# Ranks of the polynomial exponential steps, the load limit at the layer boundary and the end stop in a planned attention kernel

## Chip, cores, metric

One core of a Trainium2 chip. The metric is the device time of one execution in microseconds (us). All executions quoted are fast; a change counts as faster or slower from 2% on, and the text gives each ratio with its 95% interval. Ratios are the mean time of one kernel's fast runs over that of the kernel before in the same rounds, so not quite the ratio of the medians that are quoted.

## The reference

Two layers, each an attention block and a squared-ReLU MLP, with the same weights in both layers.

```python
B, S, D, F, H = 1, 2048, 448, 1792, 16          # Dh = 28, bf16 inputs
def attn(x):   # qkv = x @ wqkv, per head softmax(q k^T / sqrt(28)) v, then @ wo
def mlp(x):    # relu(x @ w1 + b1)**2 @ w2 + b2
x = x + attn(layernorm(x));  x = x + mlp(layernorm(x))     # layer 0
x = x + attn(layernorm(x));  x = x + mlp(layernorm(x))     # layer 1
```

## The kernel before

The kernel is written by a planner that runs at build time. Every piece of work (`Op`) has an engine, an assumed duration, dependencies and buffers; streams of such pieces have a rank. The planner takes the piece that can start first, and at equal starts the one with the smaller rank (a further rule, left out here, keeps TensorE free for scores that are due). The chip then runs each engine's pieces in that order.

```python
class Planner:
    def run(self):
        while self.streams:
            ...   # cands: (start, rank, engine, stream) of each stream's next piece
            s, _, e, st = min(cands, key=lambda c: (max(c[3][2].ready, self.clock[c[2]])
                     if c[2] == "PE" and self.turns() else c[0], c[1]))
            ...
```

Scores are cut into units of 128 keys x 512 columns: 2048 units in two layers. A group of three units goes to ScalarE's exponential. A fourth unit may be taken by VectorE, which computes the exponential by a polynomial in six steps.

```python
    def apart(i, now, us):            # may a unit go to VectorE here?
        if len(units) - i < STOP or not LEAD <= len(gbuf) <= LAST:
            return None
        ...                           # a scratch set free? a result buffer? keys ready?
        if pl.load(SPAN, "DVE") > (BB if l == 0 and qb == len(blocks[0]) - 1
                                   or l == 1 and units[i][0] < bridged else BUSY):
            return None               # BB = 0.5, BUSY = 0.95, SPAN = 12 us
        ...
    def a_unit(gi, x, src, unit, l):
        ...
        # the first step; its stream has a rank of its own, 1.5, which the change leaves
        c = Op("DVE", 0.69, take, deps=[("s", gi)], acq=sets_of(unit), rel=x)
        yield c
        pl.spawn(V_PRIO, a_rest(gi, c, box, unit, (b0, b1, b2, b3)))   # V_PRIO = 3.8
    def a_rest(gi, c, box, unit, bs):  # four polynomial steps and the power of two
        ...
```

The "row blocks" are the work on 256 rows once their attention is done: output projection, layernorm, MLP, and, in layer 0, a second layernorm and layer 1's queries, keys and values. Their stream has the rank 4 + 0.1 x block; its evictions (copies of matmul results), statistics and squares have rank 3.5.

```python
            pl.spawn(... else 4 + 0.1 * qb, chain(l, qb))
    def layernorm(...):
        ...                            # rstd on GpSimd
        nm = Op("DVE", 0.42, norm, deps=[rss[j]], ...)   # has the row block's rank
        ...                            # transposes on TensorE, then copies of xnT on VectorE
```

At the layer boundary ("the bridge") layer 1's attention starts on row blocks 0 to 2 with the keys that exist, before layer 0's last row blocks are finished; its last passes need the keys of row blocks 6 and 7.

The softmax here doesn't subtract the row's maximum and nothing guards it: scores larger than these inputs give would overflow.

## Time and profile before

| | before |
|---|---|
| median | 919.29 us when the change was predicted, 918.57 us over four runs |
| exponentials on ScalarE, units on VectorE | 652, 93 |
| start of the first and last exponential | 11.3 and 896.8 us of a span of 918.8 us |
| from the last exponential's start to the end ("tail") | 22.0 us |
| ScalarE idle in front of exponentials ("gaps") | 5.5 us |
| VectorE busy, 390 to 575 us | 120.5 us, 65% |

In a group line the columns are line, engine, operation, output and inputs, count, then busy time and mean duration in ns, then the idle time in front and who ended it. In a table by stretches each row gives the stretch, its length, and busy time and count of the engines named in the text. In a line of waits they are the piece that waited, what it waited for, the sum in us, the number of times and the longest. In a list in order of time they are start and duration in us, engine, line, operation, shapes and count; in brackets stands the idle time before.

### The profile page before, as it was taken

The page shows a single profiled execution, that of the slowest core. Times are in us where ns is not written, and L with a number is a line of the kernel's source. Part 1 is how long each engine was busy: PE and PEld are TensorE (multiplying, and loading weights), DVE is VectorE, ACT ScalarE, POOL GpSimd, SP SyncE. Part 2 cuts the span into 40 slices and gives each one's busy share as a digit, 9 for nine tenths or more (in the row PEclk, how much of TensorE's full clock was granted, in tenths as well). Part 3 has the DMA queues.
Part 4 walks back from the last instruction along what each step waited for, and adds up shares of the span by engine and source line. Part 5 has one row for each costly group of instructions (what it writes and reads, how often), then busy time and mean ns, then how long its engine had stood idle before and what let it go on. Part 6 is the DMA issues. An engine that isn't in the chain of part 4 may idle for free.

```text
span 918.8 us, 30455 instructions
## 1 busy us (share of the span) xinstructions
PE 842.7 (92%) x13606; PEld 483.0 (53%) x13606; DVE 698.9 (76%) x1433; ACT 887.3 (97%) x672; POOL 42.6 (5%) x89
## 2 busy tenths in 40 slices
PE   8999988999989999899999999888989999899998
PEld 4555545455455455455555455545445545555565
DVE  7755589799799788986667556788898978998454
ACT  5999999999999999999999999999999999999992
POOL 5100000000000000000000100000000000000000
PEclk9999999999999999999999999999999999999999
DMA  7200010000000000000000000011000000000100
GB/s 219 73 2 2 2 35 24 14 9 14 15 13 9 14 14 8 14 14 2 1 2 2 2 1 2 3 39 38 20 13 14 24 20 15 22 14 19 28 6 22
DMA packets 32992, 18.53 MB, mean 20 GB/s; under 512 B 17498, under 2 KB 32411, under 8 KB 32860
## 3 DMA queue, kind: packets, MB, share of 16 engines
q1 hardware_dynamic: 32860, 16.58, 6.3%
q8 instruction: 106, 1.74, 0.8%
q14 instruction: 26, 0.21, 0.1%
HBM read 14.26 MB, written 2.07 MB: 18 GB/s over the span
## 4 chain that ended last, share of the span: by engine, by line
ACT 66%; issue 13%; PE 11%; DVE 6%; DMA 3%; SPq 0%; POOL 0%; POOLq 0%; ACTq 0%
ACT pt L769 66%; PE mt L523 4%; PE sc L751 3%; DMA dn<-oT_sb 3%; PE oT L909 2%; PE sc L523 1%; DVE v_h L837 1%; DVE st L416 1%; DMA V_sb<-in_A_wqkv_dram 1%; DVE K_sb L837 1%; PE tp L462 0%; DVE xn L489 0%; DVE oT_sb L933 0%; DVE v_e L832 0%; DVE v_i L822 0%
## 5 line engine op out<-in xcount | busy, mean ns | idle before, releaser
L769 ACT ACTIVATE pt<-sc 128x1536 bf16<-128x1536 f32 x652 | 876.7, 1616 | 5.5 <-PE sc L751 4.0
L751 PE MATMUL sc<-Q_sb,K_sb 32*128 32x256 bf16 (+1 forms) x6288 | 334.5, 266 | 57.9 <-ACT pt L769 54.1
L751 PEld LDWEIGHTS <-K_sb 32*128 32x128 bf16 x6598 | 172.8, 92 | 228.8 <-issue 221.9
L909 PE MATMUL oT<-pt,V_sb 128*32 128x256 bf16 (+1 forms) x4164 | 150.3, 269 | 1.1 <-ACT pt L769 0.5
L909 PEld LDWEIGHTS <-V_sb 128*32 128x32 bf16 x4352 | 93.2, 96 | 47.2 <-issue 41.3
L523 PE MATMUL mt<-xnT,w 128*128 128x256 bf16 (+1 forms) x888 | 114.9, 271 | 1.1 <-DVE rec L960 0.3
L523 PEld LDWEIGHTS <-w 128*128 128x128 bf16 x952 | 79.8, 98 | 31.4 <-issue 22.3
L1041 DVE TENSOR_SCALAR r<-mt 128x512 bf16<-128x512 f32 x105 | 72.0, 686 | 24.4 <-PE mt L523 23.8
L837 DVE SCALAR_TENSOR_TENSOR K_sb<-K_sb 128x512 f32<-128x512 uint16 x132 | 90.1, 683 | 0.4
L837 DVE SCALAR_TENSOR_TENSOR v_h<-v_h,v_i 128x512 f32<-128x512 f32 x98 | 66.7, 681 | 0.3
L1003 DVE TENSOR_TENSOR x_sb<-x_sb,mt 128x448 bf16<-128x448 bf16 (+2 forms) x63 | 38.1, 605 | 27.1 <-PE mt L523 26.6
L1092 PE MATMUL mt<-xn,ident 128*128 128x448 bf16 x154 | 51.8, 356 | 3.4 <-DVE v_i L822 1.1
L523 PE MATMUL mt<-w,h 128*128 128x448 bf16 x224 | 51.9, 354 | 0.0
L751 PE MATMUL mt<-Q_sb,K_sb 32*128 32x256 bf16 x310 | 49.3, 270 | 0.8 <-DVE x_sb L1003 0.8
L438 POOL TENSOR_TENSOR ve<-mv,eps_t 128x2 f32<-128x2 f32 (+1 forms) x34 | 9.2, 272 | 858.9 <-DVE mv L417 858.9
L822 DVE TENSOR_SCALAR v_i<-mt 128x512 int32<-128x512 f32 x49 | 33.7, 687 | 16.4 <-PE mt L751 16.1
L523 PE MATMUL mt<-w,V_sb 128*128 128x448 bf16 (+2 forms) x210 | 45.0, 342 | 0.0
L416 DVE BATCH_NORM_STATS2 st<-x_sb 128x6 f32<-128x448 bf16 x64 | 39.6, 619 | 1.3 <-DMA x_sb<-in_A_x_dram 0.7
L931 DVE COPY oT_sb<-oT 128x256 f32<-128x256 f32 (+1 forms) x48 | 19.1, 397 | 27.7 <-PE oT L909 27.6
L822 DVE TENSOR_SCALAR K_sb<-mt 128x512 int32<-128x512 f32 x44 | 30.1, 685 | 10.7 <-PE mt L751 10.6
L837 DVE SCALAR_TENSOR_TENSOR v_h<-v_i 128x512 f32<-128x512 uint16 x49 | 33.5, 685 | 0.5
L541 DVE TENSOR_SCALAR Q_sb<-mt 128x512 bf16<-128x512 f32 (+1 forms) x31 | 21.0, 678 | 16.4 <-PE mt L523 16.4
(97 smaller groups left out, 736.4 us busy)
## 6 DMA issues: line engine op xcount, KB each, us to landing
rec<-scr SPq DMA_DIRECT2D x56, 128.0 KB
x_sb<-in_A_x_dram SPq DMA_DIRECT2D x8, 224.0 KB
out_dram<-x_sb SPq DMA_DIRECT2D x15, 112.0 KB
w<-in_B_w_dram SPq DMA_DIRECT2D x1, 1568.0 KB
w<-in_B_w_dram SPq DMA_DIRECT2D x1, 1344.0 KB
dn<-oT_sb SPq DMA_DIRECT2D x56, 4.0 KB
scr<-dn SPq DMA_DIRECT2D x56, 4.0 KB
V_sb<-in_A_wqkv_dram SPq DMA_DIRECT2D x1, 672.0 KB
```

What stands on the lines that cost most here:

```text
L416: nc.vector.bn_stats(out=st[:, :], in_=x_sb[:, t0 + j, :])
L523: nc.tensor.matmul(box["t"][:, c0:c0 + n], lhsT=lhsT() if callable(lhsT) else lhsT, rhs=rhs, start=a, stop=b)
L541: nc.vector.tensor_scalar(out=dst, in0=src, scalar1=by, scalar2=None, op0=ALU.mult)
L751: nc.tensor.matmul(dst[k][:, i * nt * P:(i + 1) * nt * P], lhsT=K_sb[l][rows, g, (kb + i) * P:(kb + i + 1) * P], rhs=Q_sb[rows, g, t0 * P: ...
L769: nc.scalar.activation(out=pt[:, 0:n], in_=gbuf[gi]["sc"][:, 0:n], func=AF.Exp, scale=float(np.log(2.0)) * 2.0 ** -FRAC)
L822: nc.vector.tensor_scalar(out=box["i"], in0=two(src), scalar1=EXP_BIAS, scalar2=EXP_LOW, op0=ALU.add, op1=ALU.max)
L837: nc.vector.scalar_tensor_tensor(out=box["h"], in0=box["f"] if begin else box["h"], scalar=b, in1=box["f"], op0=ALU.add, op1=ALU.mult)
L909: nc.tensor.matmul(box["t"][DHP * hh:DHP * hh + DHP, 0:n], lhsT=V_sb[l][:, kb + i, 4 * g + hh, :], rhs=p[:, c0:c0 + n], start=begin and kb ...
L931: nc.vector.tensor_copy(out=dst, in_=src)
L1003: nc.vector.tensor_tensor(out=x_sb[:, tb, lo:hi], in0=x_sb[:, tb, lo:hi], in1=t[:, 0:hi - lo], op=ALU.add)
L1041: nc.vector.tensor_scalar(out=r[:, 0:w], in0=t[:, 0:w], scalar1=0.0, scalar2=None, op0=ALU.max)
L1092: nc.tensor.matmul(t[:, 0:D], lhsT=ident[:, :], rhs=xns[0][:, 0:D], start=True, stop=True)
```

## The change

Its intent: let VectorE take more units where it is half idle, at the layer boundary (BB, the limit on VectorE's planned load over the last 12 us) and near the end (STOP, the number of units before the end from which on VectorE takes none), and keep their polynomial steps from delaying the row blocks: rank 6 instead of 3.8, and 3.0 once a unit is 5 us old.

```diff
-BB = 0.5
+BB = 0.95
-V_PRIO = 3.8
+V_PRIO = 6.0
+V_LATE = 3.0
+V_WAIT = 5.0
-STOP = 120
+STOP = 80
...  (sort and candidates accept a rank that is a function of time)
-        pl.spawn(V_PRIO, a_rest(gi, c, box, unit, (b0, b1, b2, b3)))
+        pl.spawn(lambda now: V_LATE if now > c.end + V_WAIT else V_PRIO, a_rest(gi, c, box, unit, (b0, b1, b2, b3)))
```

More of the change, by code (lines that the diff above doesn't have):

```diff
@@ L129, in spawn @@
         self.streams.append([prio, gen, next(gen, None)])
-        self.streams.sort(key=lambda s: s[0])
+        self.streams.sort(key=lambda s: s[0](0.0) if callable(s[0]) else s[0])
     def earliest(self, o):
@@ L163, in run @@
                 if s is not None:
-                    cands.append((s, st[0], e, st))
+                    cands.append((s, st[0](s) if callable(st[0]) else st[0], e, st))
             assert cands, "no stream can go on"
```

## The prediction

> **What bounds the kernel now.** I read the busy shares first, then the chain of waits, then the groups of instructions, then a table by stage. The page's first part and its chain:
>
> ```profile
> PE 842.7 (92%) x13606; PEld 483.0 (53%) x13606; DVE 698.9 (76%) x1433; ACT 887.3 (97%) x672; POOL 42.6 (5%) x89
> ...
> ACT 66%; issue 13%; PE 11%; DVE 6%; DMA 3%; SPq 0%; POOL 0%; POOLq 0%; ACTq 0%
> ```
>
> ScalarE is busy for 887.3 of 918.8 us and is most of the chain. TensorE's 92% is not an equal rival: the kernel itself fills TensorE's gaps with repeated score matmuls and throw-away matmuls to keep its clock up. The groups say what ScalarE does:
>
> ```profile
> L769 ACT ACTIVATE pt<-sc 128x1536 bf16<-128x1536 f32 x652 | 876.7, 1616 | 5.5 <-PE sc L751 4.0
> L751 PE MATMUL sc<-Q_sb,K_sb 32*128 32x256 bf16 (+1 forms) x6288 | 334.5, 266 | 57.9 <-ACT pt L769 54.1
> L822 DVE TENSOR_SCALAR v_i<-mt 128x512 int32<-128x512 f32 x49 | 33.7, 687 | 16.4 <-PE mt L751 16.1
> L822 DVE TENSOR_SCALAR K_sb<-mt 128x512 int32<-128x512 f32 x44 | 30.1, 685 | 10.7 <-PE mt L751 10.6
> ```
>
> 652 exponentials of three 128x512 units each sit nearly end to end, idle only 5.5 us in front of them. Line 822 is the first step of a unit that VectorE exponentiates instead, by a polynomial: 49 + 44 = 93 units. The sum closes: two layers of 16 heads and 8x8 units are 2048; 2048 - 93 = 1955; 1955 / 3 = 651.7.
>
> In the stage 140 to 390 us there are 187 exponentials, so one per 250 / 187 = 1.337 us (the mean of 1616 ns contains overlap of neighbours). **One unit more on VectorE therefore takes 1.337 / 3 = 0.445 us from ScalarE**, as long as ScalarE stays fed. Outside this there are a head of 11.3 us before the first exponential and a tail of about 20.6 us after the last (it starts at 896.8 us).
>
> The change touches where such units are taken, so I cut the span at the stages: 107-140, steady layer 0, last row block of layer 0, the bridge (layer 1's attention begins while layer 0's last row blocks are unfinished), its end, steady layer 1, the end. First all engines, then line 822 alone:
>
> ```profile
> 140.00:390.00 250.00, 227.01 (x3727) 129.33 (x3727) 219.31 (x444) 249.97 (x187) 9.65 (x18) 1.00 0.05 13
> 390.00:450.00 60.00, 57.82 (x828) 32.22 (x829) 43.12 (x81) 60.00 (x46) 2.75 (x6) 1.00 0.03 7
> 450.00:575.00 125.00, 119.30 (x1806) 66.82 (x1807) 77.40 (x149) 125.00 (x94) 4.29 (x12) 1.00 0.01 2
> 575.00:640.00 65.00, 55.06 (x978) 31.83 (x976) 51.50 (x114) 62.34 (x47) 1.30 (x2) 0.97 0.11 27
> 640.00:842.00 202.00, 186.30 (x2982) 103.38 (x2975) 175.87 (x355) 202.00 (x152) 6.75 (x10) 1.00 0.07 18
> ```
>
> ```profile
> 140.00:390.00 250.00, 26.25 (x39) 1.00 0.05 13
> 390.00:450.00 60.00, 1.38 (x2) 1.00 0.03 7
> 450.00:575.00 125.00, 3.45 (x5) 1.00 0.01 2
> 575.00:640.00 65.00, 6.86 (x10) 0.97 0.11 27
> 640.00:842.00 202.00, 21.28 (x31) 1.00 0.07 18
> 842.00:862.00 20.00, 0.00 (x0) 1.00 0.08 19
> ```
>
> The columns after the two of the window are busy time and count of PE, weight loads, DVE, ACT and POOL (in the second table DVE alone). Steady stages take 39 units in 250 us and 31 in 202 us, about 3.1 per 20 us, with DVE 87 to 88% busy. At the boundary (390-575) only 7 units are taken in 185 us, DVE is 65% busy (120.5 of 185), and ScalarE is 100% busy: that is the load limit BB = 0.5 at work. After 842 us none are taken: the stop.
>
> **What the Trainium skill says.** "Perfetto Trace Analysis", section Identifying the Most-Contended Engine, says that busy share is a fair measure for the Vector and Scalar engines and that the fullest engine should be improved first; here that is ScalarE at 97%, and the chain agrees. "ScalarE: Activation LUTs", section What ACT_TABLE_LOAD costs, gives 186 ns + 0.833 ns per element for an ACTIVATE with immediate operands and an overlap of some 93 ns back to back: an estimate of 1.37 us for 1536 columns, against 1.337 us here. "TensorE: Matmul & The Clock Gate", section Architectural detail, calls the ScalarE and VectorE queues strict FIFO: the order written at build time is the order run, so a rank in the planner can make one engine wait for another; the trace has one such case at 625 us, below. No page bears on the ranks themselves.
>
> **The change part by part.** No operation is removed or added as such; a planner at build time decides order and number.
>
> 1. *BB 0.5 to 0.95.* A unit's steps on VectorE are 0.686 + three of 0.683 + 0.416 + 0.683 = 3.83 us by the durations of the groups; starts in a row are 0.60 us apart where the duration is 0.68 (the next one overlaps), so it occupies about 3.4 us. Idle time of DVE in 390-575 is 185 - 120.5 = 64.5 us; at a limit of 95% about 55 us can be used, so at most 16 units. Scratch sets bound it too: the last row block of layer 0 has one set, the bridge two. At the steady rate of 3.1 per 20 us, 185 us would give 29 units against 7, so idle time is the tighter bound. Not every slot is usable: TensorE has to have a bank free and the two shared banks also serve the row blocks. I take **+13 units, from 5 to 20**: -5.8 us.
> 2. *STOP 120 to 80.* 40 more units of scores may offload: 40 / 3 x 1.337 = 18 us more, at the end from 842. DVE is 11.2 of 20 us busy there. At 3.1 per 20 us that is 2.8: **+3 units**, -1.3 us.
> 3. *V_PRIO 3.8 to 6, and 3.0 once a unit is 5 us old.* The planner picks by earliest start and uses rank only on a tie. Evictions, statistics and squares (rank 3.5) were ahead of the polynomial already; newly ahead are the normalisations (64 of 0.40 us) and the copies of the transposed blocks (33, of 0.68 or 0.42 us) with ranks of 4 and up. They no longer wait behind one or two steps of 0.60 us: perhaps 2 us per layernorm, which shortens the row blocks' chain, not ScalarE's. A late unit, on the other hand, overtakes evictions. Units have latencies over 5 us already: one taken at 615 us is closed at 625. So sets come free at about the old pace. **Units in the steady stages: 0, from -6 to +6.**
>
> Sum: 13 + 3 + 0 = 16 units, 16 x 0.445 = 7.1 us less. Then I give back 0.8 us for waits of TensorE on late polynomial results and for ScalarE gaps in the bridge's end. 919.3 - 7.1 + 0.8 = **913.0 us**.
>
> **The rivals.**
> - *The bridge is bound by the row blocks, not ScalarE.* Layer 1's last keys are cast at 571 and 577.7 us, and the passes that use them begin near 575: no room. If exponentials get there 5.8 us sooner and the keys do not, ScalarE waits and part 1 is worth nothing. For it: TensorE 95% busy in the bridge. Against it: of 816 score matmuls recorded there about 94 x 6 + 5 x 2 = 574 are needed, so 242, or 40 rounds of about 0.22 us, are filling: 9 us of room with another 1.8 of throw-away matmuls; and part 3 advances the row blocks in the 140-390 stage, where DVE is tight. Full loss would leave about 918 us.
> - *Late polynomial results hold TensorE.* At 625 us TensorE waits 1.4 us for a close step, and ScalarE then sits idle. ScalarE lacks 2.7 us of 65 in 575-640. With more units in flight, five more such waits would be 7 us and leave 919. Against it: the late rank is there to stop it, and such waits sum to only a few us now.
> - *VectorE frees more than I think.* If units go through faster by the late rank and the steady stages take 3.6 per 20 us, that is 10 units more there, 4.5 us: 908.5.
> - *The tail grows* because the last row blocks yield to polynomial steps up to 862 us. DVE is half idle there, so I expect at most 1 us.
>
> **Range and chances.** Good case: 20 + 5 + 4 units = 29, 12.9 us less, no give-back: 906.4. Bad case: 5 + 2 - 4 = 3 units, 1.3 us, with 1 us of new waits: 919. I cut a little from both ends: 907 to 918.5. Faster by over 2% is below 900.9 us, which needs 41 units more with nothing given back, beyond DVE's idle time at the boundary: 3%. Slower by over 2% is above 937.7 us and needs a planning accident of 18 us: 1.5%. Within 2%: 95.5%.
>
> **What would show it.** Line 769 should count near 647 (652 - 16/3), line 822 near 109, of which near 20 in 390-575 (7 before), 3 after 842. DVE busy in 390-575 should rise from 65% towards 85%; ScalarE should still be 100% busy there. In the steady stages line 822 stays near 39 and 31. The spacing of the exponentials stays 1.337 us. Wrong would be: the same number of units in the boundary (bank or set bound), or ScalarE idle near the bridge's end for longer than the 2.7 us of now (row-block bound), or more time in which TensorE waits for line 843.

## The result

After: 909.9 us median (909.58 to 910.8, 4 runs) against 918.57 us; ratio 0.9909, 95% interval 0.9887 to 0.993: by the 2% rule the same, but clear of no change. The prediction of 913.0 us, range 907 to 918.5, holds the result. The page of the changed kernel (line numbers are up by two):

```profile
PE 837.1 (92%) x13730; PEld 481.4 (53%) x13730; DVE 738.4 (81%) x1511; ACT 882.5 (97%) x668; POOL 42.6 (5%) x89
...
L771 ACT ACTIVATE pt<-sc 128x1536 bf16<-128x1536 f32 x648 | 871.9, 1604 | 5.5 <-PE sc L753 3.4
...
L824 DVE TENSOR_SCALAR v_i<-mt 128x512 int32<-128x512 f32 x58 | 39.7, 684 | 11.3 <-PE mt L753 11.3
L824 DVE TENSOR_SCALAR K_sb<-mt 128x512 int32<-128x512 f32 x48 | 32.9, 686 | 17.3 <-PE mt L753 17.1
```

and the first and last exponential, before and after (shortest, median and longest in ns, then first and last start):

```profile
L769 ACT ACTIVATE pt<-sc x652: 1267/1617/1840, 11.3 to 896.8; 128x1536 bf16<-128x1536 f32 x163
L771 ACT ACTIVATE pt<-sc x648: 885/1618/1849, 11.0 to 890.9; 128x1536 bf16<-128x1536 f32 x162
```

ScalarE is as full as before, with four exponentials fewer and the same 5.5 us of gaps. VectorE has 58 + 48 = 106 units, 13 more. The same stretches as in the prediction, all engines (PE, weight loads, DVE, ACT, POOL), for the boundary:

```profile
390.00:450.00 60.00, 55.67 (x863) 31.71 (x859) 54.60 (x102) 59.97 (x46) 2.19 (x4) 1.00 0.03 7
450.00:575.00 125.00, 115.37 (x1866) 64.33 (x1863) 96.91 (x187) 125.00 (x95) 4.13 (x12) 1.00 0.01 2
575.00:640.00 65.00, 56.79 (x1031) 33.12 (x1024) 57.27 (x128) 64.50 (x49) 2.27 (x4) 1.00 0.11 28
```

and of the first polynomial step alone (VectorE):

```profile
140.00:390.00 250.00, 24.01 (x35) 0.99 0.05 13
390.00:450.00 60.00, 6.16 (x9) 1.00 0.03 7
450.00:575.00 125.00, 9.59 (x14) 1.00 0.01 2
575.00:640.00 65.00, 6.85 (x10) 1.00 0.11 28
640.00:842.00 202.00, 19.85 (x29) 1.00 0.07 19
842.00:862.00 20.00, 1.38 (x2) 1.00 0.08 18
```

In 390-575 us there are 23 units for 7, VectorE is 82% busy (151.5 of 185 us) for 65%, and ScalarE is still full. The steady stages have fewer: 35 for 39, 29 for 31. Of the 10.4 us between the two profiled spans (918.8 and 908.4), 5.9 lie before the last exponential's start (896.8 to 890.9) and 4.5 in the tail (22.0 to 17.5). The first part is four exponentials of 1.345 us (876.7 / 652), 5.4 us, and a head 0.3 us shorter. The medians differ by 8.7, not 10.4 us; the profiled run of before was at the slow end of its fast runs (920.54 us).

So the fewer exponentials carried some 6 us (7.1 were forecast, for 16 units instead of 13), and a tail that nobody had forecast carried the rest. What a comparison of the two profiles cannot tell is which part of the change did what, and whether the ranks, to which the prediction gave no time at all, were needed.

### The profile page after: what moved, and what is told of

Read it like the earlier page. It is cut to its first block, busy times and chain, and to the rows that moved or that the text cites.

```text
span 908.4 us, 30788 instructions
## 1 busy us (share of the span) xinstructions
PE 837.1 (92%) x13730; PEld 481.4 (53%) x13730; DVE 738.4 (81%) x1511; ACT 882.5 (97%) x668; POOL 42.6 (5%) x89
## 4 chain that ended last, share of the span: by engine, by line
ACT 56%; PE 23%; issue 12%; DVE 6%; DMA 3%; POOL 0%; SPq 0%; ACTq 0%; DVEq 0%
ACT pt L771 56%; PE mt L525 9%; PE sc L753 7%; PE oT L911 4%; DMA dn<-oT_sb 3%; PE sc L525 1%; DVE v_h L839 1%; PE mt L1094 1%; DVE K_sb L839 1%; DVE st L418 1%; DVE xn L491 0%; PE mt L753 0%; PE tp L464 0%; DVE dn L977 0%; DVE oT_sb L935 0%
## 5 line engine op out<-in xcount | busy, mean ns | idle before, releaser
L771 ACT ACTIVATE pt<-sc 128x1536 bf16<-128x1536 f32 x648 | 871.9, 1604 | 5.5 <-PE sc L753 3.4
L839 DVE SCALAR_TENSOR_TENSOR K_sb<-K_sb 128x512 f32<-128x512 uint16 x144 | 98.4, 683 | 1.5
L1043 DVE TENSOR_SCALAR r<-mt 128x512 bf16<-128x512 f32 x105 | 72.0, 685 | 13.9 <-PE mt L525 13.0
L839 DVE SCALAR_TENSOR_TENSOR v_h<-v_h,v_i 128x512 f32<-128x512 f32 x116 | 79.0, 681 | 0.3
L753 PE MATMUL mt<-Q_sb,K_sb 32*128 32x256 bf16 (+1 forms) x384 | 58.3, 265 | 0.9 <-DVE x_sb L1005 0.9
L1005 DVE TENSOR_TENSOR x_sb<-x_sb,mt 128x448 bf16<-128x448 bf16 (+1 forms) x62 | 37.6, 607 | 17.7 <-PE mt L525 17.7
L1094 PE MATMUL mt<-xn,ident 128*128 128x448 bf16 x140 | 48.5, 359 | 2.5 <-DVE xn L491 1.3
L824 DVE TENSOR_SCALAR v_i<-mt 128x512 int32<-128x512 f32 x58 | 39.7, 684 | 11.3 <-PE mt L753 11.3
L525 PE MATMUL mt<-w,V_sb 128*128 128x448 bf16 (+1 forms) x210 | 46.7, 346 | 0.0
L839 DVE SCALAR_TENSOR_TENSOR v_h<-v_i 128x512 f32<-128x512 uint16 x58 | 39.5, 682 | 0.3
L491 DVE TENSOR_SCALAR xn<-x_sb,mv,rstd 128x448 bf16<-128x448 bf16 x64 | 25.4, 418 | 9.5 <-POOL rstd L441 9.2
```

Source lines behind the costliest of these rows:

```text
L491: nc.vector.tensor_scalar(out=xn[:, 0:D], in0=x_sb[:, t0 + j, :], scalar1=mv[0][:, j, 0:1], scalar2=ln[j], op0=ALU.subtract, op1=ALU.mult)
L525: nc.tensor.matmul(box["t"][:, c0:c0 + n], lhsT=lhsT() if callable(lhsT) else lhsT, rhs=rhs, start=a, stop=b)
L753: nc.tensor.matmul(dst[k][:, i * nt * P:(i + 1) * nt * P], lhsT=K_sb[l][rows, g, (kb + i) * P:(kb + i + 1) * P], rhs=Q_sb[rows, g, t0 * P: ...
L771: nc.scalar.activation(out=pt[:, 0:n], in_=gbuf[gi]["sc"][:, 0:n], func=AF.Exp, scale=float(np.log(2.0)) * 2.0 ** -FRAC)
L824: nc.vector.tensor_scalar(out=box["i"], in0=two(src), scalar1=EXP_BIAS, scalar2=EXP_LOW, op0=ALU.add, op1=ALU.max)
L839: nc.vector.scalar_tensor_tensor(out=box["h"], in0=box["f"] if begin else box["h"], scalar=b, in1=box["f"], op0=ALU.add, op1=ALU.mult)
```

## The experiments

Three theories went in. Theory 1: the time is the number of exponentials (1.36 us each, which is 885.5 us from first to last start over 651 intervals) plus the row-block matmuls left after the last score matmul (2400 columns per us, the rate that the planner assumes; in the trace of the kernel before, each matmul of 448 columns more in a row adds 0.19 us, an estimate of 2360 per us). Theory 2: the ranks are what makes the boundary usable. Theory 3: the number of exponentials alone. The counts that the expectations call "built" were read from each built program's instruction lists before it ran. The results (exponentials, gaps and tail are those of each profiled run):

| run | ranks | BB | STOP | exponentials / units | gaps | tail | median, us | ratio to before |
|---|---|---|---|---|---|---|---|---|
| before | old | 0.5 | 120 | 652 / 93 | 5.5 | 22.0 | 918.6 | 1 |
| the change | new | 0.95 | 80 | 648 / 106 | 5.5 | 17.5 | 909.9 | 0.9909 |
| E1 | old | 0.95 | 120 | 648 / 106 | 30.8 | 20.8 | 938.7 | 1.0204 |
| E2 | old | 0.5 | 80 | 651 / 95 | 3.2 | 25.9 | 921.3 | 1.0024 |
| E3 | new | 0.5 | 120 | 651 / 96 | 4.5 | 24.6 | 919.3 | 0.9997 |
| E4 | old | 0.95 | 80 | 646 / 110 | 33.1 | 21.7 | 938.6 | 1.0203 |
| E5 | new | 0.5 | 80 | 650 / 98 | 4.4 | 21.0 | 915.2 | 0.9969 |
| E6 | new | 0.95 | 120 | 649 / 102 | 4.0 | 18.1 | 911.9 | 0.9932 |
| E7 | new, never late | 0.95 | 80 | 646 / 110 | 9.3 | 20.8 | 914.2 | 0.9955 |
| E8 | new | 0.95 | 60 | 647 / 107 | 3.9 | 23.7 | 913.6 | 0.9945 |
| E9 | new in layer 0's blocks 0-6 only | 0.95 | 80 | 647 / 107 | 10.7 | 21.6 | 920.8 | 1.0030 |
| E10 | new after these only | 0.95 | 80 | 647 / 107 | 25.0 | 21.0 | 933.0 | 1.0171 |
| E11 | old | 0.7 | 80 | 649 / 103 | 15.1 | 20.3 | 924.5 | 1.0076 |
| E12 | new, NEAR = 7 | 0.9 | 80 | 647 / 109 | 2.5 | 18.1 | 906.9 | 0.9890 |

E1 to E4 ran in one job (before 919.18 us, 11 runs), E5 to E8 in one (before 917.99), E9 to E12 in one (before 918.08), each on another chip; all gave correct results. With the kernel before and the change, E1 to E6 are all eight combinations of the three parts. By the 2% rule every run is the same as before, except E1 and E4, whose intervals reach over 2% and are unclear; what is argued below rests on the intervals of the ratios and on the traces.

The second term of Theory 1 holds only roughly: 35200 columns left went with a tail of 17.5 us (the change), 35008 with 20.3 (E11), 41600 with 23.7 (E8) and 45632 with 21.7 (E4).

**E1, the load limit alone.**

```diff
-BB = 0.5
+BB = 0.95
```

> BB = 0.95 alone, ranks and stop as before. The built program has 106 units on VectorE (before 93), 648 exponentials (652), of the 13 more units 4 in the last row block of layer 0 and 11 in the bridge, 2 fewer in layer 1; after the last score matmul 37056 columns of matmul are left (42112). Theory 1, count and end order: 1.36 us per exponential and 1 us per 2400 columns left at the end: -5.4 - 2.1, about 911 us with ScalarE still 100% busy in the bridge. Theory 2, the ranks are what makes the boundary usable: without them ScalarE waits for layer 1's last keys near 575 us, 916 to 918 us. Theory 3, the count alone: 913 us.

938.7 us, interval of the ratio 1.0182 to 1.0227: 19.5 us slower than before, with exactly the units and exponentials of the whole change. No theory had this size. The waits of ScalarE name it:

```profile
ACT pt L769 <- PE mt L751: 27.6, 3, 23.1
```

and the order of time of ScalarE shows where:

```profile
569.35 7.07 ACT L769 ACTIVATE pt<-sc 128x1536 bf16<-128x1536 f32 x5
580.17 1.45 ACT L769 ACTIVATE pt<-sc 128x1536 bf16<-128x1536 f32 x1 [3.76 <-PE mt L751]
604.74 2.79 ACT L769 ACTIVATE pt<-sc 128x1536 bf16<-128x1536 f32 x2 [23.11 <-PE mt L751]
```

Two gaps, 3.8 and 23.1 us. The same stretch of the whole change is one line, 32 exponentials without a gap:

```profile
569.30 43.35 ACT L771 ACTIVATE pt<-sc 128x1536 bf16<-128x1536 f32 x32
```

What ended the long gap are layer 1's last keys, those of row block 7; they come in two casts, each for half of the heads. (The gap of 3.8 us ended with row block 6's keys, cast at 578.92 us.) The two casts in E1 (VectorE):

```profile
602.63 0.69 DVE L545 CAST K_sb<-mt 128x512 bf16<-128x512 f32 x1 [1.53 <-PE mt L523]
606.91 0.68 DVE L545 CAST K_sb<-mt 128x512 bf16<-128x512 f32 x1
```

in the kernel before:

```profile
570.96 0.69 DVE L545 CAST K_sb<-mt 128x512 bf16<-128x512 f32 x1
577.68 0.69 DVE L545 CAST K_sb<-mt 128x512 bf16<-128x512 f32 x1 [1.27 <-PE mt L523]
```

and after:

```profile
573.33 0.68 DVE L547 CAST K_sb<-mt 128x512 bf16<-128x512 f32 x1
580.06 0.69 DVE L547 CAST K_sb<-mt 128x512 bf16<-128x512 f32 x1
```

In E1 the last keys are some 30 us later than before (570.96 to 602.63 us for the first cast, which ended the wait; 577.68 to 606.91 for the second), and the exponentials stand. Why they are late can be read from VectorE's order in E1 between the two halves of one layernorm:

```profile
560.52 0.39 DVE L489 TENSOR_SCALAR xn<-x_sb,mv,rstd 128x448 bf16<-128x448 bf16 x1
560.82 0.68 DVE L837 SCALAR_TENSOR_TENSOR K_sb<-K_sb 128x512 f32<-128x512 uint16 x1
561.43 0.42 DVE L832 TENSOR_SCALAR v_e<-K_sb 128x512 int16<-128x512 int16 x1
...
573.30 0.69 DVE L837 SCALAR_TENSOR_TENSOR v_h<-v_h,v_i 128x512 f32<-128x512 f32 x1
573.90 0.39 DVE L489 TENSOR_SCALAR xn<-x_sb,mv,rstd 128x448 bf16<-128x448 bf16 x1
```

The second normalisation, 0.39 us of work, comes 13.4 us after the first. In between VectorE has no gap: it runs the steps of four units in two scratch sets and four evictions of attention results, so that something is ready whenever the engine is free, and at rank 3.8 a polynomial step goes ahead of rank 4 and up every time. Over E1's six layernorms from 425 to 562 us the second normalisation comes 2.4 to 13.4 us after GpSimd has the scale (rstd) that it needs, 8.0 us in the mean; in the kernel before, over the same stretch, at most 2.9 us. That is a queue in which the lowest class starves, not a wait of one or two steps.

**E2, the end stop alone.**

```diff
-STOP = 120
+STOP = 80
```

> STOP = 80 alone. Built: 95 units, 651 exponentials, 50304 columns left after the last score matmul (42112). Theory 1: -1.4 + 3.4, about 920.5 us, slower than before in spite of two more units. Theories 2 and 3 (more units on VectorE can only help, end order does not matter): 917 us.

921.3 us, ratio 1.0024 (1.0004 to 1.0045): slightly slower with two units more. The exponentials end sooner (last start 892.9 against 896.8), but the tail is 25.9 us against 22.0. So Theory 3, the count alone, does not hold; the tail grew by 3.9 us, near the 3.4 of Theory 1.

**E3, the ranks alone.** The diff of the change without BB and STOP:

```diff
-V_PRIO = 3.8
+V_PRIO = 6.0
+V_LATE = 3.0
+V_WAIT = 5.0
```

> The ranks alone, BB = 0.5 and STOP = 120 as before. Built: 96 units, 651 exponentials, 41152 columns left at the end. Theory 1: -1.4 - 0.4, about 916.7 us. Theory 2: the row blocks' shorter chain shows by itself as shorter ScalarE gaps at 575-640 and a shorter tail, 914 us or less. Theory 3: 917 us.

919.3 us, ratio 0.9997 (0.9976 to 1.0018): nothing. Both Theory 2's "914 or less" and Theory 1's 916.7 missed. But the row blocks did move: the last keys are cast at 546.77 us, 31 us before the 577.68 of the kernel before:

```profile
546.77 0.69 DVE L547 CAST K_sb<-mt 128x512 bf16<-128x512 f32 x1 [0.68 <-PE mt L525]
```

ScalarE had not been waiting for them, so nothing came of it; the ranks made slack that BB = 0.5 does not spend, and the tail happened to be 2.6 us longer.

Where the 31 us come from is seen in a layernorm of the steady stage, long before. Before the change, GpSimd's rstd and the two normalisations that need it:

```profile
244.40 0.69 POOL L439 TENSOR_TENSOR rstd<-ve,mhalf 128x2 f32<-128x2 f32 x1
250.42 0.39 DVE L489 TENSOR_SCALAR xn<-x_sb,mv,rstd 128x448 bf16<-128x448 bf16 x1
260.85 0.39 DVE L489 TENSOR_SCALAR xn<-x_sb,mv,rstd 128x448 bf16<-128x448 bf16 x1
```

and with the new ranks, in the whole change:

```profile
234.40 0.69 POOL L441 TENSOR_TENSOR rstd<-ve,mhalf 128x2 f32<-128x2 f32 x1
235.14 0.70 DVE L491 TENSOR_SCALAR xn<-x_sb,mv,rstd 128x448 bf16<-128x448 bf16 x2
```

Taking rstd and normalisations pairwise in order, the second normalisation starts 1.4, 7.0, 5.7, 4.5, 15.8, 1.5, 9.6 and 6.5 us after rstd's end in the first eight layernorms after 140 us of the kernel before, 6.5 us in the mean; in the change at most 1.0 us, 0.65 in the mean. The second key casts of successive row blocks are at 203, 274, 339 and 397 us before (71, 65 and 58 us apart) and at 197, 250, 304 and 358 us in E3 (53 to 54 apart).

**E4, the change without its ranks.**

```diff
-V_PRIO = 6.0   (and the late rank)
+V_PRIO = 3.8
```

> The change without its ranks: BB = 0.95 and STOP = 80 with V_PRIO 3.8. Built: 110 units, 646 exponentials, four units and two exponentials better than the whole change, but 45632 columns left after the last score matmul (whole change 35200, before 42112). Theory 1: -8.2 + 1.5, about 912 us, slower than the whole change by some 2 us. Theory 2: 916 us or more, ScalarE idle for over 3 us in 575-640. Theory 3: 910 us or less, as fast as the whole change or faster.

938.6 us, ratio 1.0203 (1.0178 to 1.0228). It has four units more than the whole change and loses some 28 us to it (each against the kernel before of its own job). Theory 1 and Theory 3 are refuted as whole explanations: a term for the wait on the last keys belongs in the sum.

**E5, the load limit undone.**

```diff
-BB = 0.95
+BB = 0.5
```

> The change with BB back at 0.5. Built: 98 units, 650 exponentials, 40256 columns left after the last score matmul. Theory 1 (1.36 us per exponential, 1 us per 2400 columns left): -2.7 - 0.8 from before, about 915 us. Theory 2 (the ranks are the gain): near the whole change, 911 us. Theory 3 (count alone): 916 us.

915.2 us, ratio 0.9969 (0.995 to 0.9989). With no gap in the bridge Theory 1's sum fits (915). The load limit is worth 0.6% of the 0.9%, but only on top of the ranks: without them it costs 2% (E1, E4).

**E6, the end stop undone.**

```diff
-STOP = 80
+STOP = 120
```

> The change with STOP back at 120. Built: 102 units, 649 exponentials, 35200 columns left, the same tail as the whole change. Theory 1: -4.1 - 2.9, about 911.5 us, one exponential (1.4 us) behind the whole change. Theory 3 (count alone): 914.5 us.

911.9 us, ratio 0.9932 (0.9917 to 0.9948), against 0.9909 for the change in another job: the direction and about the size of Theory 1 (one exponential, 1.4 us), though the two intervals overlap. The short tail is still there (18.1 us), so it is not the stop's doing.

**E7, no late rank.**

```diff
-V_LATE = 3.0
+V_LATE = 6.0
```

> The change with the late rank taken away: steps of the polynomial stay at rank 6 however old the unit is. Built: 110 units, 646 exponentials, 40256 columns left. Theory 1: -8.2 - 0.8, about 909.5 us, as the whole change. Rival, late results hold TensorE: without the late rank TensorE waits longer for the closing step and ScalarE idles, 912 us or more, with more than 5 us of TensorE waiting for the closing line.

914.2 us, ratio 0.9955 (0.9938 to 0.9972), some 4 us behind the change, with two exponentials fewer. The account from the profiles: 3.8 us more of gaps (9.3 against 5.5), 3.3 us more tail, 2.7 us less for two exponentials, which is 4.4; the spans differ by 4.0. The rival's time was right, its sign was not: TensorE shows no wait for the closing line at all. The largest new gap, 3.5 us at 222 us, follows a product that takes two polynomial results, the later one closed at 219.0 us; that the plan held the scores back for it is likely but not shown.

One more thing was seen on this program without running another. Leaving V_PRIO at 3.8 and lowering the row blocks' ranks to 3.6 + 0.01 x block instead, with the rest as here, builds the same instructions in the same order on every engine. So it is the relative rank of these two that acts, and nothing else about the number 6.

**E8, a still later stop.**

```diff
-STOP = 80
+STOP = 60
```

> The change with STOP = 60: the same plan up to 80 units before the end, then one unit more. Built: 107 units, 647 exponentials, but 41600 columns left after the last score matmul against 35200. Theory 1: -1.4 + 2.7 against the whole change, about 911.5 us; the last exponential starts 1.4 us sooner and the tail after it is 2 to 4 us longer. Theory 3 (count alone): 1.4 us faster than the whole change, 908.5 us.

913.6 us, ratio 0.9945 (0.9928 to 0.9963). The last exponential starts at 889.0 us, 1.9 us sooner than in the change, and the tail is 23.7 us, 6.2 us longer. Up to 80 units before the end the plan is the same; one unit more tips the order of the last row blocks. So the change's short tail hangs on the order in which the last pieces fall, and is not a property of any of its parts.

**E9 and E10, the ranks in the steady stage alone and everywhere else alone.**

```diff
-        pl.spawn(lambda now: V_LATE if now > c.end + V_WAIT else V_PRIO, ...)
+        top = V_PRIO if l == 0 and passes[unit[0]][1] < 7 else 3.8      # E10: "if not (...)"
+        low = V_LATE if l == 0 and passes[unit[0]][1] < 7 else 3.8
+        pl.spawn(lambda now: low if now > c.end + V_WAIT else top, ...)
```

> The whole change, but the new ranks hold only for units taken in layer 0's row blocks 0 to 6 (the steady stage); in the last row block, the bridge and layer 1 the polynomial has its old rank 3.8. Built: 107 units, 647 exponentials. If the row blocks lose their time in the steady stage alone, the last keys are ready in time and ScalarE has no long gap: 910 to 912 us. If the boundary's own polynomial steps delay them too, ScalarE waits some 5 to 10 us for the last keys: 916 to 920 us.

> The reverse of the run before: the steady stage of layer 0 keeps the old rank 3.8, everything after it has the new ranks. Built: 107 units, 647 exponentials. If the delay is piled up in the steady stage (before: 65 to 71 us from one row block's keys to the next instead of 53.4), the last keys are late whatever the boundary does: a ScalarE gap of 10 to 20 us near 575, 925 to 933 us. If the boundary alone matters: 912 us.

E9: 920.8 us, ratio 1.0030 (1.0017 to 1.0043). E10: 933.0 us, ratio 1.0171 (1.0153 to 1.0189). ScalarE's largest waits, first E9, then E10:

```profile
ACT pt L771 <- PE mt L753: 8.3, 1, 8.3
```

```profile
ACT pt L771 <- PE mt L753: 20.9, 3, 19.6
```

The last keys come at 588.29 and 602.83 us. Both places count, the steady stage more: the row blocks bring a backlog out of it, and the boundary's own units add to it.

**E11, half the easing with the old ranks.**

```diff
-BB = 0.5          -STOP = 120
+BB = 0.7          +STOP = 80
```

> Half the easing without the ranks: BB = 0.7, STOP = 80, V_PRIO 3.8. Built: 103 units, 649 exponentials, 35008 columns left at the end. If the old ranks leave the bridge no slack at all, each unit more there costs time: a ScalarE gap of about 10 us and some 923 us, between before and the run with 0.95. If there is a threshold above 0.7, no gap: about 911 us.

924.5 us, ratio 1.0076 (1.0057 to 1.0096). One gap of 11.5 us, the last keys at 593.72 us. With the old ranks and STOP = 80 the cost grows with the limit: 0.5 costs 0.2% (E2), 0.7 costs 0.8%, 0.95 costs 2% (E4). At 0.7 and at 0.95 the additional units at the boundary made the keys late and ScalarE wait for them.

**E12, a try for a better version.**

```diff
-BB = 0.95         -NEAR = 9
+BB = 0.9          +NEAR = 7
```

> A try for a better version: the whole change with BB = 0.9 and NEAR = 7 (the distance, in units ahead of a pass's first product, at which a row block's small matmul groups have to leave the two shared banks). Built: 109 units, 647 exponentials, 33216 columns left after the last score matmul against 35200. By one exponential (1.4 us) and 2000 columns (0.8 us) it should be 1 to 2 us faster than the change, about 908.5 us; if its three more units in the bridge and layer 1 bring new waits, no gain.

906.9 us, ratio 0.9890 (0.9872 to 0.9909): 1.1% faster than before. Its gaps are the smallest of all (2.5 us), with 109 units. That it beats the change as well is likely (0.9890 against 0.9909) but not shown: the intervals overlap and the two were not in one job. Which of its two edits did it was not tested.

## Why the prediction was right, and which steps were not

- **The bound and the price of a unit: right.** Busy time per exponential was 1.345 us before and after (871.9 / 648), the forecast 1.337; four exponentials account for 5.4 of the 5.9 us before the last start.
- **Part 1, BB, +13 units at the boundary: right in number** (16 by the windows, 7 to 23; 15 in the program's own order), and VectorE reached 82%, "towards 85%". But the step that put "-5.8 us" on it left out the delay that these units cause to the row blocks: E1 shows that the same limit alone costs 19.5 us.
- **Part 2, STOP, +3 units: four.** Alone it is worth nothing or less (E2); on top of the rest it is 1 to 2 us (E6).
- **Part 3, the ranks: the failed step.** The prediction had the mechanism ("newly ahead are the normalisations and the copies of the transposed blocks") but sized it as "one or two steps of 0.60 us: perhaps 2 us per layernorm" and then gave it no time. Measured: 6.5 us per layernorm in the mean and up to 15.8, where 0.65 us stay with the new ranks; 31 us on the last keys (E3); and some 28 us of run time once BB is eased (E4 against the change). The mistake was to count a wait as what is running plus a little. On an engine that is 88% busy, and where a new unit can be taken before the last is closed, the lowest rank waits for all of them: four units in the layernorm of E1 above.
- **Units of the steady stages, "0, from -6 to +6": -6** (39 to 35 and 31 to 29). The total is therefore 13 units more, not 16.
- **Rival 1, the bridge bound by the row blocks: real, and mis-sized.** "Full loss would leave about 918 us" assumed that the keys stay where they are and only the gain is lost. With the old ranks the extra units push the keys back by some 30 us, and E1 stands at 938.7. The prediction's reason against it, that part 3 advances the row blocks, is what E3 and E4 show. Its "no room" was a misreading: counted in the built program, the first exponential that needs row block 7's keys is the 422nd in the kernel before, and that starts at 584.8 us in its trace, 13.9 us after the cast at 570.96 us began. In the change it is the 418th, at 580.2 us, and the cast begins at 573.33: 6.9 us are left. The keys may thus come 2.4 us later than before without a gap.
- **Rival 2, late results hold TensorE:** not seen as such in the change. Without the late rank the kernel is 4 us slower, but by gaps and tail (E7).
- **The tail: wrong in sign.** "At most 1 us" longer was forecast; 4.5 us shorter was measured. E8 shows that one unit more brings it back. This part of the gain is luck of the order as far as the runs show, and the agreement of the sum (913.0 against 909.9) owes something to it: the give-back of 0.8 us and three units too many stood against a tail that the sum did not have.

## What to carry to other kernels

When work is moved to a half-idle engine, ask first whose short pieces already queue there: a rank below a stream that always has something ready is a wait of many pieces, not of one. Slack and its use have to come together: neither the ranks (no gain) nor the load limit (2% loss) shows its worth alone, so test the pair as well as each part. When a planner orders everything, compare what is left after the bounding engine's last piece too, because one piece moved can shift the end by several us.

## What the Trainium skill lacked or had wrong

- "ScalarE: Activation LUTs", What ACT_TABLE_LOAD costs: 186 ns + 0.833 ns per element and an overlap of about 93 ns back to back give estimates of 1.466 us for a 1536-column exponential alone and of one per 1.37 us in a row. Here one between two gaps took 1.45 us (E1, at 580.17 us), near the first, and in the steady stage there was one per 1.337 us, 2.5% less than the second.
- Nothing wrong with VectorE's rate: "Vector Engine (DVE) Microarchitecture Reference", 5.2 Measured stream behaviour on trn2, gives 1.0417 ns per column and about 75 ns per instruction after overlap, an estimate of 0.61 us for 512 columns; steps recorded with 0.68 us started 0.60 us apart here.
- No page says in which order independent pieces should be put into a statically planned in-order queue, or what a wrong order costs; the runs show 13.4 us of waiting for a 0.39 us piece behind polynomial steps (E1).
